# Attention's rounds and tail, the first expert slots in a new order, and 16-bit routing tables built from pairs

## The chip, the cores and the metric

The kernel runs on one core of a Trainium2 chip. The metric is the device time of one execution in microseconds (us); three runs of the kernel before gave 990.22, 992.68 and 995.25, median 992.68. In the profile PE is TensorE (PEld its weight loads), DVE is VectorE, ACT is ScalarE, POOL is GpSimd, and SP is SyncE, which issues most of the loads.

## What is computed

Three layers follow each other. Attention over 4 batches, 8 heads of 64 and 768 positions: each chunk of 32 queries sees 16 keys to its left, itself, 8 to its right, and 8 memory keys. Its output, 3072 tokens of 512, goes to a mixture of experts with one expert per token, and that to a dense layer.

```python
scores = scale * q_c @ concat([mem_k, k_ctx]).T        # per chunk of 32 queries
a = exp(scores - scores.max(-1)); a = a / (a.sum(-1) + 1e-9)
out[chunk] = a @ concat([mem_v, v_ctx])
x = out.reshape(3072, 512)
logits = (x / (|x| + 1e-6)) @ (emb / (|emb| + 1e-6)).T / tau     # 8 experts
e = logits.argmax(1); g = softmax(logits)[e]
y = g * (relu(x @ w1[e]) @ w2[e])                      # w1 512x1024, w2 1024x512
r = relu(y @ w_in); out = (r * r) @ w_out              # w_in 512x2048
```

## The kernel before

The order of every engine's instructions is written by hand: the code emits them in the order in which each engine takes them, and each engine works through its own queue in that order. DMAs are issued by SP, POOL and ACT as instructions of their queues.

Attention runs in 32 rounds (4 batches, 4 pairs of heads, 2 halves), as a pipeline over the stages in `order`. In round i come stage_b(i), the scores in `sp` (two banks in turn); max_b, sub_b and exp_b(i); stage_c(i-1), which transposes the probabilities in `ps_t` and copies them to `pt`; stage_d(i-2), times v, in the one bank `ps_o`; inv_d and scale_d(i-2), which empty it into `xa`; stage_t(i-3), which stores a half batch to x_d at its last pair of heads, and transposes `xa`; stage_m(i-4), the logits `lp`; and stage_u(i-5), which at the last pair transposes the logits (`dp`, in `ps_t`) into `dots`. `windows` lays out keys on POOL two rounds ahead. v, k and q are loaded on SP three, five and four pairs ahead. Five more rounds without new scores end the attention.

`early` is a generator whose steps run behind the stages: after each of batches 0 to 2 it chooses an expert per token (choose, five DVE ops), then picks the fullest expert, finds its first 256 tokens by one-hot tables (`ohs`, `rid`, product `ip`) and gathers them as slots 0 and 1. `begin` loads that expert's first weights as soon as it is known. `routing` (steps "N") counts all tokens and builds the rest: positions, one-hot tables osl, rid, ohl, the ids of the other slots by the product `idp` (31 slots of 128 tokens), experts and reloads, gates ("M", "rgm", product `gp`) and scatter indices.

Products in the slots split each operand into a high part (ACT copy) and a low part (DVE subtraction), and use three matmuls. Letters in the strings given to `run` name steps: W splits a weight block, x transposes and splits tokens, a and b are the two halves of the first product (12 matmuls each, with ReLU on ACT), c and d transpose their results, e and f are the halves of the second product, G gathers, V renews a weight block if the expert changes, F scales and scatters a slot, q takes squares of x for the norm, p is a quarter of an opened a.

```python
x0 x1 q | A0 p q W1 q | p q p q | N q q q p          # rounds 33 to 36; W0 in 32
N2 p9 N3 a1 c0 b0 N4 W2 d0 b1 N5 G2 G3 W3 N6 e0 c1 N6 f0 M4 d1 x2 N6 R V0 V1 G4 e1 M99 N7 f1 a2 x3 b2 N8 c2 F0 F1 V2 N9 V3 N10
```

After these a loop takes slots 2 to 27, two stages apart, with the dense layer's weights converted in between (its first steps: a3, d2, e2, c3, x4, b3, f2). The dense layer follows from about 480 us on.

Of the kernel before, what the change touches and what calls it, by code (L numbers as in the profile page):

```python
# [21 lines left out]
def kernel(  # L22
# [196 lines left out]
    def attention(actx, hooks, space, drain):  # L219
        x_p = actx.enter_context(tc.tile_pool(name="x", bufs=4))  # L220
# [100 lines left out]
        def stage_d(i):  # L321
            b, hp, half = ks[i]
            pt = st.pop(i)
            vt, c0 = vb[i // 2 % NV], i % 2 * NC
            op = ps_o.tile([P, HT, 2, D + 1], F32, name="op", tag="o")
            for c in range(NC):
                j = c % 4
                nc.tensor.matmul(
                    out=op[32 * j:32 * j + 32, c // 4],
                    lhsT=pt[:, c // 4, 32 * j:32 * j + 32],  # L330
                    rhs=vt[:, :, c0 + c, :],
                    start=True, stop=True,
                    tile_position=(0, 32 * j),
                )
            st[i] = op
# [18 lines left out]

        def stage_t(i):
            b, hp, half = ks[i]
            xa = x_t[b, half]
            if hp == HP - 1:
                T0 = (2 * b + half) * HT
                nc.gpsimd.dma_start(out=x_d[T0 * P:(T0 + HT) * P, :].rearrange("(t p) d -> p t d", p=P), in_=xa)  # L360
# [7 lines left out]
        def stage_m(i):  # L368
# [9 lines left out]
            if hp == HP - 1:  # L378
                lt = wk.tile([32 * HT, P], F32, name="lt", tag="lt", bufs=2)
                copy("a", lt, lp[half])  # L380
                st[i] = lt

        def stage_u(i):
            b, hp, half = ks[i]
            if hp == HP - 1:
                lt = st.pop(i)
                dp = ps_t.tile([P, HT, P], F32, name="dp", tag="t")[:, 0, :32 * HT].rearrange("p (t e) -> p t e", e=32)
# [39 lines left out]
        clear_kw(0, nc.vector)  # L427
        clear_kw(1, nc.scalar)
# [25 lines left out]
        cst = {"scratch": scratch}  # L454
        chores = {
            0: [
                start_en, lambda: windows(1), lambda: clear_kw(2, nc.scalar),
                lambda: [f(j) for f, j in ((load_q, 1), (load_k, 2), (load_q, 2), (load_k, 3), (load_q, 3), (load_k, 4))],
            ],
            4: [finish_en],  # L460
            8: [lambda: cst.update(routing_consts(route, per))],
        }
        later = {
            0: [lambda: clear_v(1, 0, nc.scalar), lambda: load_v(1)],
            1: [lambda: clear_v(2, 0, nc.scalar)],
            2: [lambda: clear_v(2, 1, nc.scalar), lambda: load_v(2)],
            3: [lambda: clear_v(3, 0, nc.scalar)],
            4: [lambda: clear_v(3, 1, nc.scalar), lambda: load_v(3)],
            5: [lambda: clear_v(4, 0, nc.scalar)],
            6: [lambda: clear_v(4, 1, nc.scalar), lambda: load_v(4), lambda: load_v(5)],  # L470
# [19 lines left out]
        for i in range(NK + LAG + 3):  # L490
            if i == NK:
                qk_ctx.close()
                space()
            for f in chores.get(i, []):
                f()
            for f, lag in order:
                if lag <= i < NK + lag:
                    f(i - lag)
                if stage_of(i):
                    wait[0] = next(early, None) == 1  # L500
                drain((i - NK, order.index((f, lag))))
# [12 lines left out]
            drain((i - NK, -1))  # L514
            for _ in range(min(len(squares), 1 if i < NK else 0)):
# [4 lines left out]
        while vec:  # L520
            vec.pop(0)()
        for f in squares:
            square(*f)
        for _ in early:
            pass
        return cst


    def routing_consts(pool, tmp):
        c = {}  # L530
# [3 lines left out]
        nc.vector.tensor_copy(out=c["iota"], in_=it[:, 0:NS])  # L534
        itp = tmp.tile([P, 1], I32, name="itp")
        nc.gpsimd.iota(itp, pattern=[[0, 1]], base=0, channel_multiplier=1)
        c["p"] = pool.tile([P, 1], F32, name="p_f")
        nc.vector.tensor_copy(out=c["p"], in_=itp)
        c["p1"] = pool.tile([P, 1], F32, name="p1_f")
        nc.vector.tensor_scalar(out=c["p1"], in0=c["p"], scalar1=1.0, scalar2=None, op0=ALU.add)  # L540
        c["rev"] = pool.tile([P, E], F32, name="rev")
        nc.vector.tensor_scalar(
            out=c["rev"], in0=c["iota"][:, 0:E], scalar1=-1.0, scalar2=float(E), op0=ALU.mult, op1=ALU.add
        )
        c["iota_b"] = pool.tile([P, P], BF16, name="iota_b")
        nc.vector.tensor_copy(out=c["iota_b"], in_=it)
        c["ones"] = pool.tile([P, P], BF16, name="ones_b")
        nc.vector.memset(c["ones"], 1.0)
        c["first"] = pool.tile([P, E], F32, name="first")
        nc.vector.tensor_copy(out=c["first"], in_=c["rev"])  # L550
        nc.vector.memset(c["first"][:, 0:1], float(E * 2 * NT))
        c["upper"] = pool.tile([P, P], BF16, name="upper_b")
# [3 lines left out]
        return c  # L556
# [36 lines left out]
    def early(c, per, ps, begin, gather):  # L593
# [47 lines left out]
        for T in range(TE - 1):  # L641
# [17 lines left out]
        lf = t([P, TE], BF16, "lf")  # L659
        nc.vector.scalar_tensor_tensor(  # L660
            out=lf, in0=osl[:, :, 1], scalar=-float(P), in1=pe, op0=ALU.mult, op1=ALU.add
# [19 lines left out]
        yield from gap((6, 1, 6, 1, 8, 6)[4])  # L681
# [17 lines left out]

    def routing(rp, c):  # L700
        def t(shape, dt=F32, name=None, tag=None):
            return rp.tile(shape, dt, name=name, tag=tag or name)

        def gates(g, gb):
# [20 lines left out]
            for j in range(3):  # L725
                nc.vector.tensor_copy(out=gb[j], in_=g)
                yield
                if j < 2:
                    nc.vector.tensor_tensor(out=g, in0=g, in1=gb[j], op=ALU.subtract)
# [21 lines left out]
        for _ in choose(c, rp, TE, NT):  # L751
            pass
        turn(c, rp, km[:, TE:NT].rearrange("p t o -> p (t o)"), "1")
        for _ in tally(c, rp, 1):
            pass
        g = t([P, NT, 1], name="g")
        gb = [t([P, NT, 1], BF16, name=f"gb{j}") for j in range(3)]
# [7 lines left out]
        yield  # L765
        for part in range(2):
# [49 lines left out]
        lo = t([P, NT, 1], BF16, name="lo")  # L816
        nc.vector.tensor_copy(out=lo, in_=posi)
        slot = t([P, NT, 1], name="slot")
        nc.vector.tensor_copy(out=slot, in_=sli)
        osl = t([P, NT, NS], BF16, name="osl")  # L820
        nc.vector.tensor_tensor(
            out=osl, in0=c["iota"][:, 0:NS].unsqueeze(1).to_broadcast([P, NT, NS]),
            in1=slot.to_broadcast([P, NT, NS]), op=ALU.is_equal,
        )
        rid = t([P, NT, 2, NS], BF16, name="rid", tag="rid")
        nc.vector.tensor_tensor(
            out=rid[:, :, 0, :], in0=osl,
            in1=c["iota"][:, 0:NT].unsqueeze(2).to_broadcast([P, NT, NS]), op=ALU.mult,
# [3 lines left out]
        idp = ps_r[2].tile([P, 2, NS], F32, name="idp", tag="o")  # L832
        yield
        nc.vector.tensor_tensor(
            out=ohl, in0=c["iota_b"].unsqueeze(1).to_broadcast([P, NT, P]), in1=lo.to_broadcast([P, NT, P]),
            op=ALU.is_equal,
        )
# [5 lines left out]
        nc.scalar.activation(out=idt, in_=idp[:, 0, :], func=ACTF.Copy, scale=float(P))  # L843
        nc.vector.tensor_tensor(out=ida, in0=idt, in1=idp[:, 1, :], op=ALU.add)
        nc.vector.tensor_scalar(out=gid[:, KE:NS], in0=ida[:, KE:NS], scalar1=-1.0, scalar2=0.0, op0=ALU.add, op1=ALU.max)
        rg = t([P, NT, 3, NS], BF16, name="rg")

        def rgm(j):
            nc.vector.tensor_tensor(out=rg[:, :, j, :], in0=osl, in1=gb[j].to_broadcast([P, NT, NS]), op=ALU.mult)
# [66 lines left out]
        gp = ps_r[1].tile([P, 3, NS], F32, name="gp", tag="t")  # L916
# [806 lines left out]
```

## Time and profile before

| | us |
|---|---|
| median of three runs | 992.68 |
| the profiled execution | 992.88 |
| its span, first to last instruction | 991.2 |
| PE busy | 952.7 (96%) |
| DVE busy | 622.8 (63%) |
| ACT busy | 396.8 (40%) |
| POOL busy | 161.4 (16%) |

The mean granted clock of TensorE is 0.991 of its full speed. "Busy" is the time in which an engine works at all; the time between the span and the execution's own time, 1.7 us, is start and end. The stretches in which the change lies are the first sixth of the span: the rounds up to the start of round 29 (91.49), the end of attention up to the first expert product (113.64), and the first slots up to slot 2's second product (160.58).

### The profile page before, as it was taken

Reading aid. Unit: us, or ns where it says so; the run is one execution under the profiler, and the core shown is the slowest. Engines: PE = TensorE matmul, PEld = TensorE weight load, DVE = VectorE, ACT = ScalarE, POOL = GpSimd, SP = SyncE. Lnnn points to the kernel's source line nnn. Section 1 sums busy time; section 2 is a strip of 40 time slices with the busy share of each in tenths; the row PEclk is TensorE's granted clock in tenths of the full one; section 3 lists DMA queues with packets and bytes.
Section 4 is the critical chain, followed back from the end, with each engine's and each line's share of the span. In section 5 each row is a group of like instructions: output and inputs, shape, how many; then the busy total and the mean of one; then the engine's idle time right before and its main releaser. Section 6 shows DMA issues by size and latency. Waiting matters only on the chain.

```text
span 991.2 us, 17171 instructions
## 1 busy us (share of the span) xinstructions
PE 952.7 (96%) x5982; PEld 775.9 (78%) x5982; DVE 622.8 (63%) x1259; ACT 396.8 (40%) x731; POOL 161.4 (16%) x197
## 2 busy tenths in 40 slices
PE   6889799999999999999899999999999999999997
PEld 5767577888887887878688888878888888888886
DVE  7778795647757677877798645555454555444522
ACT  7656533635546465666432213421111341111221
POOL 8765212121211111110000001010000101000011
PEclk9999899999999999999999999999999999999999
DMA  8994716554857676896565434032454204224011
GB/s 322 350 411 146 254 42 229 193 166 130 309 183 280 210 276 239 317 342 233 184 203 192 161 123 143 1 110 85 145 191 146 88 1 151 91 100 148 1 43 43
DMA packets 62496, 172.94 MB, mean 174 GB/s; under 512 B 7092, under 2 KB 7220, under 8 KB 62400
## 3 DMA queue, kind: packets, MB, share of 16 engines
q1 hardware_dynamic: 43392, 122.45, 35.5%
q0 software_dynamic: 8640, 28.32, 8.0%
q10 hardware_dynamic: 10368, 20.98, 6.2%
q8 instruction: 49, 0.80, 0.3%
q14 instruction: 47, 0.39, 0.1%
HBM read 213.66 MB, written 38.80 MB: 255 GB/s over the span
## 4 chain that ended last, share of the span: by engine, by line
issue 66%; DMA 15%; POOL 2%; POOLq 0%
DMA y_d<-ysb,sidx 15%; POOL out_dram L1382 2%; POOLq L1719 0%; POOLq L1031 0%; POOLq L1382 0%; POOLq L1157 0%; POOLq L1656 0%; POOLq L1665 0%
## 5 line engine op out<-in xcount | busy, mean ns | idle before, releaser
L1357 PE MATMUL acc<-wo,g 128*128 128x512 f32 x384 | 151.2, 394 | 0.2
L1359 PE MATMUL acc<-wo,g 128*128 128x512 f32 x384 | 151.0, 393 | 0.0
L1358 PE MATMUL acc<-wo,g 128*128 128x512 f32 x384 | 149.5, 389 | 0.0
L1382 POOL DMA_INDIRECT out_dram<-osb,oid x24 | 23.6, 983 | 483.9 <-ACT osb L1378 355.9
L1359 PEld LDWEIGHTS acc<-wo,g 128*128 128x128 f32 x384 | 72.1, 188 | 17.3 <-DVE g L108 1.3
L1357 PEld LDWEIGHTS acc<-wo,g 128*128 128x128 f32 x384 | 72.1, 188 | 16.5 <-ACT g L105 1.5
L1358 PEld LDWEIGHTS acc<-wo,g 128*128 128x128 f32 x384 | 72.2, 188 | 16.0
L1402 DVE SCALAR_TENSOR_TENSOR cf<-cf 128x512 f32<-128x512 f32 x54 | 37.1, 692 | 75.7 <-ACT cf L1425 74.9
L1157 POOL DMA_INDIRECT y_d<-ysb,sidx x28 | 32.2, 1150 | 273.4 <-ACT ysb L1156 214.7
L105 ACT CAST g<-cf 128x512 fp32r<-128x512 f32 x54 | 33.6, 622 | 106.9 <-PE acc L1359 71.0
L1425 ACT COPY cf<-zX 128x512 f32<-128x512 f32 x24 | 14.1, 586 | 155.2 <-PE zX L1336 155.2
L1336 PE MATMUL zX<-yc,ww 128*128 128x512 f32 x192 | 68.8, 399 | 2.3 <-DVE tu L1291 2.3
L108 DVE TENSOR_TENSOR g<-gk,g 128x512 fp32r<-128x512 f32 x42 | 29.1, 692 | 66.3 <-ACT g L105 66.3
L1336 PE MATMUL zW<-yc,ww 128*128 128x512 f32 x192 | 68.2, 396 | 0.4 <-PEq L1665 0.4
L1336 PE MATMUL zY<-yc,ww 128*128 128x512 f32 x192 | 67.7, 393 | 0.0
L105 ACT CAST g<-gk 128x512 fp32r<-128x512 f32 x42 | 26.2, 623 | 79.8 <-PE acc L1359 79.8
L108 DVE TENSOR_TENSOR g<-cf,g 128x512 fp32r<-128x512 f32 x54 | 37.4, 692 | 29.8 <-ACT g L105 28.9
L135 POOL COPY kw<-kt 64x672 f32<-64x672 f32 x62 | 51.3, 828 | 10.2 <-PE sp L277 7.8
L108 DVE TENSOR_TENSOR hTlb<-tr,hThb 128x512 fp32r<-128x512 f32 x28 | 19.3, 690 | 44.0 <-ACT hThb L105 43.6
L1108 PE MATMUL yps<-wh2a,hTha 128*128 128x512 f32 x112 | 46.2, 413 | 0.0
L1336 PEld LDWEIGHTS zX<-yc,ww 128*128 128x128 f32 x192 | 36.6, 190 | 10.9 <-ACT ysb L1156 2.7
L1108 PE MATMUL hps<-wh1b,xT 128*128 128x512 f32 x104 | 43.2, 415 | 1.8 <-ACT ha L1125 1.8
(328 smaller groups left out, 2281.2 us busy)
## 6 DMA issues: line engine op xcount, KB each, us to landing
ww<-wi_d SPq DMA_DIRECT2D x77, 512.0 KB
r1a<-in_moe_w_dram SPq DMA_DIRECT2D x54, 512.0 KB
r1b<-in_moe_w_dram SPq DMA_DIRECT2D x54, 512.0 KB
r2a<-in_moe_w_dram SPq DMA_DIRECT2D x52, 512.0 KB
r2b<-in_moe_w_dram SPq DMA_DIRECT2D x52, 512.0 KB
wi_d<-ww SPq DMA_DIRECT2D x28, 512.0 KB
vb<-in_v_dram SPq DMA_DIRECT2D x32, 390.0 KB
rw<-in_moe_w_in_dram ACTq DMA_DIRECT2D x32, 256.0 KB
```

Source lines behind the costliest of these rows:

```text
L105: nc.scalar.copy(out=hi, in_=src)
L108: eng.tensor_tensor(out=lo, in0=src, in1=hi.bitcast(F32), op=ALU.subtract)
L135: (nc.vector if eng == "v" else nc.gpsimd).tensor_copy(out=out, in_=in_)
L1108: nc.tensor.matmul(out=out_ps, lhsT=ah, rhs=wh, start=first, stop=False)
L1157: nc.gpsimd.indirect_dma_start(out=y_d[:, :], out_offset=bass.IndirectOffsetOnAxis(ap=sidx[:, s:s + 1], axis=0), in_=y, in_offset=None, bo ...
L1336: nc.tensor.matmul(out=z, lhsT=w[:, d % 2, wx, kt], rhs=y[yx][:, kt, :], start=start and (kt, x) == (0, 0), stop=(kt, x) == (1, 2), skip_g ...
L1357: nc.tensor.matmul(out=self.acc[j], lhsT=g[:, 0, c], rhs=wt[:, 0], start=first, stop=False)
L1358: nc.tensor.matmul(out=self.acc[j], lhsT=g[:, 0, c], rhs=wt[:, 1], start=False, stop=False)
L1359: nc.tensor.matmul(out=self.acc[j], lhsT=g[:, 1, c], rhs=wt[:, 0], start=False, stop=last)
L1382: ins = nc.gpsimd.indirect_dma_start(out=out[:, :], out_offset=bass.IndirectOffsetOnAxis(ap=oid[:, jj:jj + 1], axis=0), in_=o, in_offset=N ...
L1402: nc.vector.scalar_tensor_tensor(out=o, in0=x, scalar=0.0, in1=x, op0=ALU.max, op1=mul)
L1425: nc.scalar.copy(out=c1[:, 0], in_=z)
```

## The change

In the rounds, the choices for batches 0 and 1 run one step per round instead of one per stage; the constants of the routing become a generator, two steps a round; `dp` goes to the pool of `lp`; v of pair 1 is loaded ahead of four other loads and v of pairs 2 to 5 one round earlier; six x tiles instead of four, and batch 1 is stored after rounds 27 and 28. Stage_d of round 30 uses `sp`'s first bank. Attention's last rounds are written out, with the weights' high (h, j, H) and low parts (l, k, L) as steps of their own, and transposes (X, C, D) apart from their splits (Y and y, g, i). One-hot tables read index and position as pairs of 16-bit words, and their inner width grows from 31 to 32. The first slots come in a new order: b0 and b2 have PSUM banks of their own, `gp` comes behind d2, and y2 has its bank held ahead. Slot 3's a and slot 2's d move out of the loop into the string.

```diff
-            sp = (ps_s, ps_s2)[i % 2].tile([P, HT, 64, 2], F32, name="sp", tag="s")
+            sp = (ps_s, ps_s2)[i % 2].tile([P, HT, D + 1, 2], F32, name="sp", tag="s")[:, :, 0:64]
-            op = ps_o.tile([P, HT, 2, D + 1], F32, name="op", tag="o")
+            pool, tag = (ps_s, "s") if i == NK - 2 else (ps_o, "o")
+            op = pool.tile([P, HT, 2, D + 1], F32, name="op", tag=tag)
-                dp = ps_t.tile([P, HT, P], F32, name="dp", tag="t")[:, 0, :32 * HT].rearrange(...)
+                dp = ps_l.tile([P, HT, 32], F32, name="dp", tag="l")
+        clear_v(1, 0, nc.scalar)
-                lambda: [f(j) for f, j in ((load_q, 1), (load_k, 2), (load_q, 2), (load_k, 3), (load_q, 3), (load_k, 4))],
+                lambda: [f(j) for f, j in ((load_q, 1), (load_k, 2), (load_v, 1), (load_q, 2), (load_k, 3), (load_q, 3), (load_k, 4))],
+            27: [lambda: store(1, 0)],
+            28: [lambda: store(1, 1)],
-            return not wait[0]
+            return not wait[0] and (i >= starts[-1] or f is stage_u)
+                if i > 4 and f is stage_u:
+                    for _ in range(2):
+                        next(consts, None)
+                if (i, f) == (NK - 1, stage_c):
+                    drain("h0")
...
+        L = NK - 1
+        drain("h1")
+        stage_d(L - 1)
+        for _ in range(3):
+            next(early)
+        stage_m(L - 3); stage_c(L); stage_t(L - 2); inv_d(L - 1); scale_d(L - 1)
+        drain("l0 q q")
+        stage_d(L); stage_m(L - 2); stage_t(L - 1); inv_d(L); scale_d(L)
+        drain("l1 j0")
+        stage_m(L - 1, False); stage_t(L)
+        drain("X0")
+        for _ in early: pass
+        finish_m(L - 1); stage_m(L); stage_u(L - 1)
+        drain("Y0")
+        stage_u(L)
+        drain("y0")
+        # choose, turn and tally of the last batch
+        drain("N q q j1 A0 p2 X1 k0 Y1 y1 k1 q p9 q")
...
-                out=all_ohs[:, T:T + G], in0=c["iota_b"].unsqueeze(1).to_broadcast([P, G, P]),
-                in1=lf[:, T:T + G].unsqueeze(2).to_broadcast([P, G, P]), op=ALU.is_equal,
+                out=paired(all_ohs[:, T:T + G]), in0=along(c["iota_b"], G), in1=across(lf[:, T:T + G], P),
+    def paired(t):
+        return t.rearrange("p t (a b) -> p t a b", b=2)
+    def along(row, n):
+        m = row.shape[1]
+        return row.rearrange("p (a b) -> p a b", b=2).unsqueeze(1).to_broadcast([P, n, m // 2, 2])
+    def across(col, m):
+        return col.unsqueeze(2).to_broadcast([P, col.shape[1], m // 2, 2])
-        yield from gap((6, 1, 6, 1, 8, 6)[4])
+        yield from gap(12)
...
+            pool, tag = {(0, "b"): (self.ps_y, "y"), (2, "b"): (ps_r[0], "s")}.get((s, ab), (self.ps_h, self.tags[0]))
-        run("N2 p9 N3 a1 c0 b0 N4 W2 d0 b1 N5 G2 G3 W3 N6 e0 c1 N6 f0 M4 d1 x2 N6 R V0 V1 G4 e1 M99 N7 f1 a2 x3 b2 N8 c2 F0 F1 V2 N9 V3 N10")
+        run("N a1 c0 H20 H21 b0 N L20 L21 N b1 d0 e0 C1 H30 H31 L30 N G2 G3 L31 g1 f0 D1 N i1 e1 N x2 N R f1")
+        run("V0 V1 G4 a2 M12 x3 M99 b2 N c2 N V2 a3 d2 N O2 F0 F1 V3 N N")
```

The tables osl, rid, ohl and rg use `paired`, `along` and `across` in the same way.

## Rows read from the trace of the kernel before

**Rows 1.** Busy us and count of each engine by stretch, PEclk, DMA share, GB/s.
```profile
0.00:91.49 91.49, 76.75 (x1666) 60.84 (x1666) 69.57 (x230) 62.29 (x134) 68.59 (x109) 1.00 0.88 333
91.49:113.64 22.15, 15.65 (x306) 12.31 (x305) 18.45 (x61) 11.43 (x27) 5.26 (x8) 0.92 0.46 156
113.64:160.58 46.94, 42.02 (x248) 32.40 (x248) 38.92 (x113) 18.83 (x37) 6.06 (x8) 0.93 0.49 168
160.58:480.00 319.42, 312.92 (x1544) 259.17 (x1543) 225.64 (x409) 181.93 (x316) 57.43 (x51) 1.00 0.69 239
480.00:991.20 511.20, 505.38 (x2224) 411.19 (x2223) 270.20 (x449) 122.28 (x221) 24.05 (x25) 0.99 0.32 107
```
**Rows 2.** PE's waits from 0 to 91.49: total us, times, longest.
```profile
PE op L328 <- issue: 2.4, 3, 1.2
PE op L328 <- ACT xt L133: 1.3, 1, 1.3
PE dp L388 <- ACT pt L133: 1.2, 5, 0.2
PE op L328 <- DVE mx L293: 1.1, 1, 1.1
PE op L328 <- DVE sp L288: 0.7, 1, 0.7
```
**Rows 3.** Timeline of weight loads near 19.7: start, us, operation, idle before and releaser.
```profile
19.71 0.63 PEld L328 LDWEIGHTS op<-vb,pt 128*32 128x32 f32 x24 [1.31 <-ACT xt L133]
```
**Rows 4.** Stretches of 5 us in the rounds, columns of rows 1.
```profile
60.00:65.00 5.00, 3.85 (x69) 2.71 (x66) 3.48 (x10) 2.94 (x10) 4.70 (x8) 1.00 1.02 412
...
80.00:85.00 5.00, 5.00 (x121) 4.11 (x120) 3.88 (x12) 3.35 (x9) 3.78 (x6) 1.00 0.52 193
```
**Rows 5.** Timeline of DVE: first and last operation of the first choice.
```profile
44.17 0.20 DVE L563 TENSOR_REDUCE mxl<-dots 128x6 f32<-128x48 f32 x1
...
45.95 0.47 DVE L611 TENSOR_TENSOR e_o<-rev,km 128x48 bf16<-128x48 f32 x1
```
**Rows 6.** DVE groups from 91.49 to 160.58: busy us, mean ns, idle before.
```profile
L834 DVE TENSOR_TENSOR ohl<-iota_b,lo 128x3072 bf16<-128x3072 bf16 x1 | 3.3, 3348 | 0.0
...
L669 DVE TENSOR_TENSOR scratch<-iota_b,e_lf 128x768 bf16<-128x768 bf16 x3 | 2.8, 950 | 0.1
L849 DVE TENSOR_TENSOR rg<-osl,gb 128x744 bf16<-128x744 bf16 x3 | 2.6, 927 | 0.0
L108 DVE TENSOR_TENSOR wl1a<-r1a,wh1a 128x1024 fp32r<-128x1024 f32 x2 | 2.4, 1224 | 1.9 <-ACT wh1a L105 1.9
L108 DVE TENSOR_TENSOR wl1b<-r1b,wh1b 128x1024 fp32r<-128x1024 f32 x2 | 2.4, 1223 | 2.2 <-ACT wh1b L105 2.2
...
L826 DVE TENSOR_TENSOR rid<-osl,iota_f 128x744 bf16<-128x744 bf16 x1 | 0.9, 939 | 0.0
...
L830 DVE TENSOR_SCALAR rid<-osl,p_f 128x744 bf16<-128x744 bf16 x1 | 0.4, 406 | 0.0
```
**Rows 7.** Timeline of PE in attention's end and the first slots.
```profile
104.35 1.52 PE L328 MATMUL op<-vb,pt 128*32 128x130 f32 x24 [1.08 <-ACT xt L133]
...
151.50 0.69 PE L1108 MATMUL hps<-wh1b,xT 128*128 128x512 f32 x1 [1.82 <-ACT ha L1125]
...
155.96 1.23 PE L918 MATMUL gp<-rg,ohl 128*128 128x93 bf16 x24
...
160.58 0.48 PE L1108 MATMUL yps<-wh2a,hTha 128*128 128x512 f32 x1
```
**Rows 8.** DVE's busy us from the end of round 31 to the gate tables.
```profile
104.25:155.49 51.24, 42.38 (x120) 0.90 0.47 157
```
**Rows 9.** PE's waits from 91.49 to 160.58, as in rows 2.
```profile
PE hps L1108 <- ACT ha L1125: 2.6, 2, 1.8
...
PE xp L363 <- DVE spare L108: 1.7, 1, 1.7
PE ip L684 <- DVE e_rid L680: 1.3, 1, 1.3
```

More of the change, by code (lines that the diff above doesn't have):

```diff
@@ L353, in square, with store @@
             nc.scalar.activation(out=sq, in_=x_t[b, half][:, t, :], func=ACTF.Square, accum_out=ssq[:, T:T + 1])
+        def store(b, half):
+            T0 = (2 * b + half) * HT
+            nc.gpsimd.dma_start(out=x_d[T0 * P:(T0 + HT) * P, :].rearrange("(t p) d -> p t d", p=P), in_=x_t[b, half])
         def stage_t(i):
@@ L357, in stage_t @@
             xa = x_t[b, half]
-            if hp == HP - 1:
-                T0 = (2 * b + half) * HT
-                nc.gpsimd.dma_start(out=x_d[T0 * P:(T0 + HT) * P, :].rearrange("(t p) d -> p t d", p=P), in_=xa)
+            if hp == HP - 1 and b != 1:
+                store(b, half)
             tp = ps_a.tile([P, HT, P], F32, name="xp", tag="a")
@@ L366, in stage_t, with finish_m, stage_m @@
             st[i] = xt
-        def stage_m(i):
+        def finish_m(i):
+            lt = wk.tile([32 * HT, P], F32, name="lt", tag="lt", bufs=2)
+            copy("a", lt, lp[ks[i][2]])
+            st[i] = lt
+        def stage_m(i, finish=True):
             b, hp, half = ks[i]
@@ L377, in stage_m @@
                 )
[L378 to L381, printed above, removed]
+            if hp == HP - 1 and finish:
+                finish_m(i)
         def stage_u(i):
@@ L489, in attention @@
         cst["square"] = lambda: square(*squares.pop(0)) if squares else None
[L490 to L493, printed above, removed]
+        for i in range(NK):
             for f in chores.get(i, []):
@@ L750, in routing @@
         stp = ps_r[1].tile([P, E], F32, name="stp", tag="t")
[L751 to L755, printed above, removed]
         g = t([P, NT, 1], name="g")
-        gb = [t([P, NT, 1], BF16, name=f"gb{j}") for j in range(3)]
+        gb = [t([P, NT, 2], BF16, name=f"gb{j}") for j in range(3)]
         gate_ops = gates(g, gb)
@@ L831, in routing @@
         ohl = t([P, NT, P], BF16, name="ohl")
-        idp = ps_r[2].tile([P, 2, NS], F32, name="idp", tag="o")
+        idp = ps_r[2].tile([P, 2, NP], F32, name="idp", tag="o")
         yield
[L834 to L837, printed above, removed]
+        nc.vector.tensor_tensor(out=paired(ohl), in0=along(c["iota_b"], NT), in1=across(lo, P), op=ALU.is_equal)
         yield
@@ L915, in routing @@
         yield
-        gp = ps_r[1].tile([P, 3, NS], F32, name="gp", tag="t")
-        for T in range(NT):
-            nc.tensor.matmul(out=gp, lhsT=ohl[:, T, :], rhs=rg[:, T], start=(T == 0), stop=(T == NT - 1))
-        nc.vector.tensor_reduce(
-            out=gate.unsqueeze(2), in_=gp.rearrange("p j s -> p s j"), op=ALU.add, axis=AX.X
-        )
         nc.vector.tensor_tensor(
@@ L946, in routing @@
         yield
-        eq = t([P, NT, NS], name="eq", tag="rid")
+        gp = ps_r[1].tile([P, 3, NP], F32, name="gp", tag="t")
+        for T in range(NT):
+            nc.tensor.matmul(out=gp, lhsT=ohl[:, T, :], rhs=rg[:, T], start=(T == 0), stop=(T == NT - 1))
+        nc.vector.tensor_reduce(
+            out=gate.unsqueeze(2), in_=gp[:, :, 0:NS].rearrange("p j s -> p s j"), op=ALU.add, axis=AX.X
+        )
+        yield
+        eq = t([P, NT, NP], name="eq", tag="rid")[:, :, 0:NS]
         nc.vector.tensor_tensor(
@@ L989, in first, with first_high, first_low @@
             self.after(kind, 0)
+        def first_high(self, i, kind="1a"):
+            nc.scalar.copy(out=self.res[kind][i][0], in_=self.raw[kind, i])
+        def first_low(self, i, kind="1a"):
+            hi, lo = self.res[kind][i]
+            nc.vector.tensor_tensor(out=lo, in0=self.raw[kind, i], in1=hi.bitcast(F32), op=ALU.subtract)
+            if i:
+                self.after(kind, 0)
         def renew(self, kind, s, eng="v"):
@@ L1103, in xtr @@
                 lo = self.sp.tile([P, KD, P], F32R, name="xTl", tag="xTl")
-            split(hi, lo, tp)
+            parts = [
+                lambda: nc.scalar.copy(out=hi, in_=tp),
+                lambda: nc.vector.tensor_tensor(out=lo, in0=tp, in1=hi.bitcast(F32), op=ALU.subtract),
+            ]
+            if apart:
+                self.parts[s] = parts
+            else:
+                for f in parts:
+                    f()
             self.xT[s] = (hi, lo)
@@ L1140, in mm2 @@
             hh, hl = self.hT.pop((s, ab))
-            if ab == "a":
+            if ab == "a" and s not in self.y:
                 pool, tag = (ffn.ps, "zW") if s % 2 and KE < s < NA - 3 else (self.ps_y if s else self.ps_y0, "y")
```

142 lines of the change are left out of this document (93 added, 49 removed).

## The prediction, made before the result was known

> **What bounds the kernel now.** I read the windows first [rows 1]. From 160.58 us on TensorE is busy all but 6.5 us of 319, at full clock, and the same holds near enough to the end: there only fewer matmuls would help, and the change takes none away. What can be gained lies ahead of 160.58, the start of slot 2's second product, a point that both orders reach with the same PE work done. PE idles 14.7 us of the 91.49 of the rounds, 6.5 of the 22.15 of attention's end and 4.9 of the 46.94 of the first slots; in the last two the mean clock is 0.92 and 0.93, so about 3.5 and 6.6 us ran at the lower of the two levels (1.2 instead of 2.4 GHz). VectorE (DVE) is the next engine there: 38.92 of 46.94 us busy.
>
> The waits of PE in the rounds [rows 2] name what holds them: the single PSUM bank of stage_d's output, which scale_d has to empty first, so that DVE's lateness shows as PE's wait (1.3 and 0.7 us); the logit transpose `dp`, which shares its bank with the probability transposes (1.2 in five places); 1.1 us under DVE `mx`, at 19.75, where the weight load ahead of it shows ACT's `xt`, long done by then [rows 3], so that I read it as the v tile still in flight; and 2.4 us of "issue" in the middle of groups of stage_d, where nothing in the profile is waited for, while the DMA engines were full [rows 4]. The 1.3 us wait comes right behind the choice: its operations begin at 44.17, the last at 45.95 [rows 5], in front of the round's max.
>
> **Part by part: the rounds.** For batches 0 and 1 the choice becomes one DVE operation at the end of each round from 12 on (the last, from round 28, stays dense), and the constants two a round. That takes 1.3 and 0.7 off [rows 2]; I count 1.8. A new op costs about 0.2 there; DVE idles 21.9 of 91.49 us [rows 1], 0.65 a round, so it hides; without that cover, ten choice steps and eleven constants would cost some 4 us. `dp` in lp's bank no longer waits for the copy of `pt`: 1.2. The v load for pair 1 goes ahead of four q and k loads on SP's in-order queue, and its zeros ahead of the first windows on ACT: 1.1, of which I count 0.9, since scale_d is next late; four q and k tiles land two transfers' time later, and bounds are a gain of 1.1 and, if one of them is then late, a loss of as much. The store of batch 1 moves on POOL's queue past some thirty window copies to rounds 27 and 28; ahead of it POOL no longer waits for scale_d, and 1.6 MB leave the stretch with a DMA share of 1.02 for one with 0.52 [rows 4]. If the "issue" gaps are late instruction loads they shrink; bounds are 0 and 2.4, and I take the middle, 1.2, because one gap coincides with a choice and one does not. Sum of the rounds: 1.8 + 1.2 + 0.9 + 1.2 = 5.1 us; bounds -1.1 and 6.6.
>
> **The tables from pairs.** Before, every table row is built at the one-element rate: 3348 ns for 3072 elements, 927 to 950 for 744 or 768 [rows 6]. No two-source operation at another rate is in this trace, so the ends are no gain and the rate of the nearest all-16-bit row, `rid` by a scalar: 744 elements in 406 ns, 44% of the two-source row. I take a half, near that row, since both read pairs of 16-bit words side by side: ohl 1.6, osl and rid 0.4 each, rg 1.2 saved of the slots, 3.6 together, and 1.2 of the three early tables.
> The Trainium skill (VectorE: DVE Perf Modes, section on the perf-mode tier table) gives two-tensor operations on 16-bit SBUF data twice the base rate and no more; by it these four groups would save the 4.8 us that I take, by the other reading nothing; no row here shows it.
>
> **Attention's end and the first slots.** The three early tables stand in front of max and sub of round 31, and the ids of the first gathers follow: 1.2 us earlier. Stage_d of round 30 gets a bank of its own and no longer waits 1.08 [rows 7]. That brings the first expert product forward by 2.3.
> From 104.25 to 155.49 DVE is one long queue, 42.38 busy of 51.24 [rows 8]. Its two largest gaps, 1.9 and 2.2, are waits for the high halves that ACT was just then making [rows 6]; now h, j and H stand far ahead of l, k and L, with other DVE work between. Off go 4.1 of gaps and 3.6 of tables. Added is the low half of x3, which moves ahead of the gates: 0.6, half of a 1024-wide row [rows 6]. DVE side: 7.1 shorter, 1.2 earlier, 8.3 in all.
> On PE the gate product `gp` waits for DVE's last tables. It stood before c2, a3 and d2, some 3.5 us of work (gp 155.96 + 1.23 to 160.58 [rows 7]); now these run while DVE finishes. DVE and order together: 11.8.
> The PE bound is lower. In 113.64 to 160.58 PE is busy 42.02; with the 6.6 us at the lower level run at full clock that is 38.7, so 8.2 can go there, and with the 2.3 ahead of it 10.5. The waits that would go are named [rows 9]: 2.6 for ReLU results in the one bank of the first products (b0 and b2 now have banks of their own), one of them the 1.82 before 151.50 [rows 7]; 1.7 for x's halves, 1.3 for `ip`. I count 9.5, a microsecond below the bound, for small waits that come back.
> What is moved in and could wait: h0 stands in front of the last exp on ACT and needs the first weights, loaded in round 30; the gathers stand ahead of the stores of batch 3 and of the 2a and 2b loads on POOL, and these come earlier with it; L20 and L21 stand in front of the one-hot table on DVE and put off the ids of gathers 2 and 3 by 2.4 (two rows of 1.22), covered by f0 and e1, which now run before x2; if that cover is short, up to 2.4 are lost. The copies of y0 and y1 come later, which only their banks feel: y2 gets one of its own.
>
> **Sum.** 5.1 + 9.5 = 14.6. The profiled execution took 992.9 (span 991.2), next to the median of 992.7: 992.9 - 14.6 = 978.3, forecast 978 us. Its own bounds: all waits of the rounds and the full PE bound give 6.6 + 10.5, 976; PE's busy time holds ends that are modelled, so I allow 4 more below.
>
> **Rivals.**
> Tables at the old rate: 4.8 comes back on DVE, 11.8 becomes 7.0, less the microsecond 6.0: 992.9 - 11.1 = 982. For it: the second source still steps by zero over the middle axis. 0.10.
> The clock falls anyway. Before 104.35 PE did a few small groups with gaps of 1.3 [rows 9] and 1.1, and the 24 small matmuls there took 1.52; at 151.50, after 1.82 idle behind a full run, a matmul took 0.69 against 0.48 at 160.58 [rows 7]. The new end of attention still goes from engine to engine, with transposes between. If the slow share stays, 3.3 of the PE bound is not recovered, and the end of attention is longer by about one: 982. The Trainium skill (TensorE: Matmul & The Clock Gate, part 4 on transposes) says that transposes do not count as busy for the clock as matmuls do; by that rule attention's end, with its many transposes, would be at the lower level; the rounds, with the same mix, show 1.00 [rows 1], which speaks against it. 0.14.
> DMA holds the rounds. With a share of 1.02 [rows 4] faster rounds may only wait for q, k and v; the rounds give 1: 982. Against: the loads run three to five pairs ahead, and the waits of the rounds show one late tile [rows 2]. 0.10.
> Two of these together: 986 to 990, mostly no change. 0.09.
> Slower: DVE becomes what the first slots wait for, and PE's gaps, each as long as the 1.82 before 151.50, recur in every block, so that the clock stays at the lower level through them. Eleven blocks of 12 matmuls by 0.21 each (0.69 - 0.48 [rows 7]) are 28 us. It decides from 70 of the 132 matmuls on, where the 14.6 are used up; at 90% of them 978 + 25 = 1003. Against it: DVE's queue is shorter than before by 7, and PE has four blocks of products between the waits. 0.07.
>
> **How the numbers follow.** The forecast has 0.50. Within 0.5% (988 to 998) is about what a measurement of this kernel can tell from no change. Faster: forecast, old table rate, clock, DMA, 0.84; the same 0.09; slower 0.07. The range 972 to 987 holds the forecast's bounds and the three single rivals and leaves out the slower one, most of the double ones and a little below.
>
> **What would show it.** Right: ohl near 1.7 us; `dp` and stage_d without waits in rounds 12 to 24; first hps near 111 on a clock of 5 us earlier, so 106 in the span; no gap of DVE over a microsecond until rg but the branch at V0; gp right behind d2; slot 2's second product starting near 146 instead of 160.58. Wrong: a wait of PE over 1.5 us behind DVE low halves after b0, granted clock 0.50 after the first hps, stage_b waiting for q or windows, or a stretch after 160.58 that is longer than before, which the sum takes as unchanged.

## The result, and the profile after

The changed kernel takes 978.24 us (median of 4, 975.62 to 983.58) against 993.81 (990.22 to 995.25): a ratio of 0.9846, 95% interval 0.9817 to 0.9875. The forecast was 978. The total came out as forecast, several of the steps under it did not. The windows of the changed kernel, cut at the same events as [rows 1] (columns as there):

```profile
0.00:87.46 87.46, 75.32 (x1666) 60.17 (x1666) 67.90 (x230) 61.71 (x133) 66.52 (x106) 1.00 0.91 339
87.46:107.26 19.80, 15.80 (x330) 11.89 (x329) 17.84 (x63) 14.06 (x33) 10.17 (x14) 1.00 0.63 219
107.26:149.67 42.41, 39.18 (x231) 31.18 (x227) 35.91 (x112) 16.41 (x32) 3.76 (x4) 0.96 0.54 185
149.67:480.00 330.33, 324.99 (x1600) 268.80 (x1597) 234.84 (x427) 185.81 (x322) 57.18 (x51) 1.00 0.67 233
480.00:976.80 496.80, 491.35 (x2171) 400.35 (x2169) 260.95 (x432) 118.65 (x213) 23.62 (x24) 1.00 0.32 109
```

Round 29's `sp` starts 4.03 us earlier (forecast 5.1), the first expert product 6.38 (107.26; forecast 106), slot 2's second product 10.91 (149.67 for 160.58; forecast 146). From there to the end of the span it is 827.1 us instead of 830.6, where the sum had no change. So 3.7 us were missing at slot 2's second product, 1.1 of them already at round 29 and 2.6 behind it (6.9 gained there, forecast 9.5), and 3.5 came back after that product.

PE's waits in the rounds, beside [rows 2] (total us, times, longest):

```profile
PE tp L316 <- ACT e L305: 1.7, 1, 1.7
PE op L329 <- ACT sq L354: 1.4, 1, 1.4
PE op L329 <- issue: 1.2, 1, 1.2
PE sp L277 <- issue: 0.9, 1, 0.9
PE op L329 <- DVE sp L288: 0.4, 2, 0.2
```

The waits of `dp` and most of those behind DVE are gone; three stalls of about a microsecond are left (under ACT `sq` and twice under "issue"; the last section says where they stand), and the wait for the first exponential (1.1 in the kernel before) is 0.6 longer, because ACT now clears 1560 words for the second v tile ahead of the first keys. The tables on DVE, beside [rows 6]:

```profile
L891 DVE TENSOR_TENSOR ohl<-iota_b,lo 128x3072 bf16<-128x3072 bf16 x1 | 1.8, 1751 | 0.0
L721 DVE TENSOR_TENSOR scratch<-iota_b,e_lf 128x768 bf16<-128x768 bf16 x3 | 1.6, 550 | 0.1
L903 DVE TENSOR_TENSOR rg<-osl,gb 128x768 bf16<-128x768 bf16 x3 | 1.5, 556 | 0.5 <-DVEq L1066 0.5
```

They run at a little over half of the old time. And PE in the first slots, from c2's transposes to slot 2's second product (start, us, operation, idle before and its releaser), where [rows 7] has 151.50 to 160.58:

```profile
140.69 0.60 PE L1211 MATMUL tr<-ident,ha 128*128 128x128 f32 x4
141.89 0.50 PE L1186 MATMUL hps<-wh1a,xT 128*128 128x512 f32 x1 [0.60 <-ACTq L1066]
143.97 0.50 PE L1187 MATMUL hps<-wl1a,xT 128*128 128x512 f32 x1 [1.58 <-DVEq L1066]
...
145.34 0.63 PE L1186 MATMUL hps<-wh1a,xT 128*128 128x512 f32 x1
...
148.67 1.18 PE L999 MATMUL gp<-rg,ohl 128*128 128x96 bf16 x24
149.67 0.47 PE L1186 MATMUL yps<-wh2a,hTha 128*128 128x512 f32 x1
```

Here is what the forecast left out. The product a3, the first of slot 3, was moved ahead of `gp`; its weights are renewed under a condition (`If`, L1066), which ACT and DVE evaluate in their queues at the place where `use` of the next product, b2, issues it. That place is behind the gate's operations (M99). PE waits 0.60 for ACT to reach it and 1.58 for DVE, though nothing is renewed (no split of the 1a weights runs on either engine there); then a matmul takes 0.63 instead of 0.39 until `gp`.

### The profile page after: what moved, and what is told of

It is laid out like the page before. It is cut to its first block, busy times and chain, and to the rows that moved or that the text cites. A ratio compares the mean times of both kernels' runs of the same rounds, so it can differ in the third digit from the quotient of the medians.

```text
span 976.8 us, 17175 instructions
## 1 busy us (share of the span) xinstructions
PE 946.6 (97%) x5982; PEld 772.4 (79%) x5982; DVE 617.4 (63%) x1260; ACT 396.6 (41%) x731; POOL 161.2 (17%) x197
## 4 chain that ended last, share of the span: by engine, by line
issue 37%; PE 12%; POOL 2%; POOLq 0%; DVE 0%; ACT 0%; ACTq 0%
PE zW L1422 2%; PE zX L1422 2%; POOL out_dram L1468 2%; PE zY L1422 2%; PE acc L1445 1%; PE acc L1443 1%; PE acc L1444 1%; PE zZ L1422 1%; POOLq L1813 0%; POOLq L1468 0%; DVE g L108 0%; ACT g L105 0%; ACTq L105 0%
## 5 line engine op out<-in xcount | busy, mean ns | idle before, releaser
L1188 PE MATMUL yps<-wh2a,hTla 128*128 128x512 f32 x112 | 44.2, 395 | 0.0
```

The lines of the kernel that those rows point to most:

```text
L1188: nc.tensor.matmul(out=out_ps, lhsT=al, rhs=wh, start=False, stop=last)
```

## Experiments

Beside each group of experiments the kernel before ran on the same chip (medians 993.55 to 994.80), and the ratios are to those runs. The points in the span, in us (e2 is the start of slot 2's second product; n is the number of timed executions):

| kernel | sp of round 29 | first hps | e2 | sp 29 to e2 | e2 to end | time | n |
|---|---|---|---|---|---|---|---|
| before | 91.49 | 113.64 | 160.58 | 69.09 | 830.6 | 993.81 | 4 |
| after | 87.46 | 107.26 | 149.67 | 62.21 | 827.1 | 978.24 | 4 |
| after_again | 86.82 | 107.27 | 147.88 | 61.06 | 827.6 | 979.75 | 4 |
| if_first | 87.22 | 107.70 | 146.57 | 59.35 | 829.4 | 978.64 | 4 |
| if_v2 | 85.78 | 106.73 | 145.91 | 60.13 | 828.8 | 976.22 | 4 |
| one_elem | 87.70 | 109.30 | 153.81 | 66.11 | 831.5 | 983.48 | 4 |
| pairs_only | 92.40 | 113.93 | 158.33 | 65.93 | 830.2 | 989.38 | 10 |
| a3_loop | 87.23 | 107.74 | 151.60 | 64.37 | 829.2 | 982.75 | 4 |
| dense | 88.96 | 109.95 | 150.65 | 61.69 | 827.0 | 979.25 | 1 |
| dp_old | 89.34 | 110.50 | 152.84 | 63.50 | 827.6 | 982.11 | 1 |
| v_late | 88.61 | 109.54 | 150.37 | 61.76 | 830.3 | 982.31 | 1 |
| op30_old | 85.93 | 107.97 | 149.94 | 64.01 | 829.6 | 981.20 | 1 |
| if_v2_vlate | 87.71 | 108.60 | 147.93 | 60.22 | 828.3 | 977.98 | 4 |
| if_v2_zeros | 86.05 | 106.50 | 145.53 | 59.48 | 828.1 | 975.83 | 4 |

Seven of these have the changed kernel's rounds unaltered (after, after_again, if_first, if_v2, one_elem, a3_loop, op30_old): their round 29 starts at 85.78 to 87.70, mean 86.88. That width is the error bar of a single profile there. Behind round 29 two profiles of the changed kernel differ by 1.15 (62.21 and 61.06).

**if_first: the branch ahead of the gate.**

```
-V0 V1 G4 a2 M12 x3 M99 b2 N c2 N V2 a3 d2 N
+V0 V1 G4 a2 M12 x3 b2 M99 N c2 N V2 a3 d2 N
```

> The changed kernel with slot 2's second half of the first layer (b2) issued ahead of the rest of the gate's operations instead of behind them, so that the conditional renewal of slot 3's 1a weights, which b2's use emits on ACT and DVE, is decided before them. Theory: of the 3.7 us by which slot 2's second product starts later than forecast (149.67 for 146), 2.2 are the two waits of slot 3's first half (0.60 on ACT's branch, 1.58 on DVE's) and 1.5 the lower clock behind them. Expected: neither wait over 0.3, granted clock 1.00 from 140 to 150, the second product at 146.0 to 147.3 (gp may now wait up to 1.4 for rg, since the gate's exponential comes behind hb on ACT), the time 975 to 976. Rival: the wait is on what the branch decides (a weight load or its flag) and not on its place in the queue; then the product stays at 149 or later and the time at 978.

Its timeline of PE, columns as above:

```profile
141.27 0.48 PE L1186 MATMUL hps<-wh1a,xT 128*128 128x512 f32 x1
141.59 0.39 PE L1187 MATMUL hps<-wl1a,xT 128*128 128x512 f32 x1
...
145.57 1.18 PE L999 MATMUL gp<-rg,ohl 128*128 128x96 bf16 x24 [0.85 <-DVE rg L903]
146.57 0.47 PE L1186 MATMUL yps<-wh2a,hTha 128*128 128x512 f32 x1
148.46 0.50 PE L1187 MATMUL yps<-wl2a,hTha 128*128 128x512 f32 x1 [1.42 <-DVEq L1066]
```

a3 loses both waits, the granted clock is 1.00 from 140 to 150, `gp` waits 0.85 for rg, and e2 is at 146.57, all as expected: the wait was the branch's place in the queue. But the time is 978.64 (ratio 0.9848, 0.9805 to 0.9890), where 975 to 976 was expected. The next branch, V2 for slot 2's 2a weights, stood behind cmpt to sidx on DVE and now holds e2's second matmul 1.42.

**if_v2: the second branch, too.**

```
-V0 V1 G4 a2 M12 x3 M99 b2 N c2 N V2 a3 d2 N
+V0 V1 G4 a2 M12 x3 b2 M99 N V2 c2 N a3 d2 N
```

> As if_first (slot 2's b2 issued ahead of the rest of the gate's operations), and the renewal of slot 2's 2a weights (V2) moved from behind the output indices (cmpt to sidx on DVE) to right behind rg. In if_first a3 lost its waits and slot 2's second product began at 146.57, but its second matmul then waited 1.42 us on DVE's branch of V2 (148.46). Theory: that branch, too, is late only by its place; expected: second matmul by 147.2 with no wait over 0.3, 1.3 us less than if_first in the second matmul's start, the clock 1.00 to 150, the time 976 to 977, or 1.3 below if_first beside it. Rival: V2's branch waits for a weight load or for its flag, and the wait stays at 148 wherever it is put (rg's reader gp then comes later, too): no gain, time as if_first or longer.

```profile
144.91 1.18 PE L999 MATMUL gp<-rg,ohl 128*128 128x96 bf16 x24 [0.86 <-DVEq L1066]
145.91 0.48 PE L1186 MATMUL yps<-wh2a,hTha 128*128 128x512 f32 x1
146.22 0.40 PE L1187 MATMUL yps<-wl2a,hTha 128*128 128x512 f32 x1
```

There is no wait behind e2, the second matmul starts at 146.22, and the time is 976.22 (0.9820, 0.9799 to 0.9841). e2 is 14.67 earlier than in the kernel before, as forecast (14.6), but 5.7 of that are a round 29 that is the earliest of the seven, 1.1 ahead of their mean. What the branches decide is the part behind round 29: the forecast gave 9.5 there, the changed kernel gains 6.9 and 8.0 (after_again), and the four kernels with the first or both branches moved gain 8.9 to 9.7.

**one_elem: tables read one element at a time, in the new order.**

```
-        return t.rearrange("p t (a b) -> p t a b", b=2)
+        return t
-        return row.rearrange("p (a b) -> p a b", b=2).unsqueeze(1).to_broadcast([P, n, m // 2, 2])
+        return row.unsqueeze(1).to_broadcast([P, n, m])
-        return col.unsqueeze(2).to_broadcast([P, col.shape[1], m // 2, 2])
+        return col[:, :, 0:1].to_broadcast([P, col.shape[1], m])
```

> The changed kernel with the tables' operands read as in the kernel before: one element held with step 0 along the inner axis instead of two (paired, along and across give plain views; types and sizes stay). Theory of the forecast: the tables go back to their full time (ohl 3.3 us, early tables 0.93 each, rg 0.9 each, rid 0.9) and DVE bounds the end of attention and the first slots, so first hps is about 1 us later and slot 2's second product 3.5 to 4.8 later (153.2 to 154.5); time 982. Rival: in the new order TensorE's own work and the branch bound that stretch, and the tables cost less than 2 us of the second product's start; time 979 to 980.

Its table of DVE groups and PE's first group behind the biggest table:

```profile
L891 DVE TENSOR_TENSOR ohl<-iota_b,lo 128x3072 bf16<-128x3072 bf16 x1 | 3.4, 3351 | 0.0
L721 DVE TENSOR_TENSOR scratch<-iota_b,e_lf 128x768 bf16<-128x768 bf16 x3 | 2.8, 947 | 0.1
```

```profile
127.73 0.87 PE L894 MATMUL idp<-rid,ohl 128*128 128x64 bf16 x24 [1.18 <-DVE ohl L891]
```

Types and sizes are those of the changed kernel, so the step-0 element alone costs the factor of two. Counted from round 29, e2 is 3.9 later than in the changed kernel (66.11 - 62.21), 5.1 later than in after_again; the time is 983.48 (0.9880, 0.9836 to 0.9923). The forecast's 4.8, of which it counted a microsecond less on the path, fits both. One profile can't say more: it is of the slowest of the four executions (986.99), with a granted clock of 0.92 from round 29 to the first hps, where the changed kernel has 1.00.

**pairs_only: the pairs alone, in the kernel before** (the helpers above, pieces, flags and tile numbers in pairs; nothing else).

> The kernel before with the pairs alone (tables' operands, gate pieces and flags in pairs; order, banks, choices and consts as before). Theory of the forecast: DVE bounds from the early tables to rg, so the 4.8 us that the tables save are all on the path: first hps 1.2 earlier (112.4), slot 2's second product 4.0 to 4.8 earlier (155.8 to 156.6), time 989. Rival: without the new order other waits (gathers, xp behind squares, ha) take the room: the product less than 2.5 us earlier, time 991 or more.

The biggest table, ohl, takes 1748 ns here, too, and e2 is 3.16 earlier from round 29 (69.09 - 65.93), 2.25 in the span. The time is 989.38 (0.9950, 0.9927 to 0.9974). The time is the first theory's, the point lies between the two. The point is mixed with the clock, too: from the first hps to e2 it is 2.5 shorter, but there the granted clock is 1.00 instead of 0.93, and PE is busy 38.42 instead of 42.02. In the old order a part of what DVE saved met another wait, stage_d's last op for `pt` (0.16 in the kernel before, at 107.75):

```profile
108.12 1.40 PE L328 MATMUL op<-vb,pt 128*32 128x130 f32 x24 [2.14 <-ACT pt L133]
```

**a3_loop: a3 and d2 behind gp again** (out of the string, and the two `if s > KE` of the loop removed).

> The changed kernel with slot 3's first half (a3) and the second transposes of slot 2 (d2) back behind gp, as in the kernel before. The forecast gave 3.5 us to this order, as work that fills gp's wait for rg. Theory: most of that was eaten by the branch: gp now waits 3 to 4 us for rg (ready near 145.5), a3 and d2 follow without a wait of their own, and slot 2's second product starts at 150 to 151 against 149.67; time 979. If the forecast's 3.5 was right the product starts at 153 or later and the time is 981.5. Rival: the branch cost more than the order gave; the product starts before 149.3 and the time is below 978.

```profile
145.82 1.89 PE L999 MATMUL gp<-rg,ohl 128*128 128x96 bf16 x24 [4.27 <-DVE rg L903]
```

`gp` waits 4.27, longer than either theory had, and its 24 matmuls take 1.89 instead of 1.18, at a granted clock of 0.66 from 145 to 150. e2 is at 151.60, between the 150 to 151 of mine and the 153 of the forecast's step; time 982.75 (0.9881, 0.9841 to 0.9922), nearer to that step's 981.5. From round 29 the order is worth 2.2 to 3.3 us with its branch wait (64.37 less 62.21 and 61.06) and 4.2 without it (less 60.13). But a part of a3_loop's own delay is the clock: from `gp` to e2 it takes 5.78, where the kernel before takes 4.25 for the same work (160.58 - 155.96, less 0.37 for c2). With these 1.5 off, an estimate, the order is worth 1.8 with its branch wait (beside after_again) and 2.7 to 3.5 without it (beside if_v2 and if_first). My theory that the branch had eaten most of it is not borne out: it took a third to a half.

**dense: choices in a row and constants at once** (`return not wait[0]`; all constants in round 8).

> The changed kernel with the choices of the first three batches in a row again and the routing constants at once in round 8, as in the kernel before. Theory of the forecast: 1.2 to 1.8 us come back as waits of op and dp behind DVE in rounds 8 to 20, round 29's sp at 88.7 to 89.3 against 87.2 to 87.5 in the three runs of the changed rounds. Rival: the other edits left DVE with room, or the waits were put down to DVE but had another cause; then less than 0.4.

```profile
47.59 0.87 PE L329 MATMUL op<-vb,pt 128*32 128x130 f32 x24 [1.53 <-ACT xt L133]
...
71.70 0.87 PE L329 MATMUL op<-vb,pt 128*32 128x130 f32 x24 [1.85 <-ACT xt L133]
```

Round 29 starts at 88.96, 1.3 to 3.2 behind the seven, 2.1 behind their mean: as forecast (1.2 to 1.8), within what one profile tells. The first stall stands at the same product as the 1.35 of the kernel before (48.54), behind the choice of batch 0. The second stands behind the choice of batch 1, one round later than a stall of 1.25 under "issue" in the kernel before (71.09). The row names ACT's xt, but DVE's division xa, which empties op's one bank and comes behind the choice in DVE's queue, ends at 71.60 (71.04 and 0.56), and op starts at 71.70.

**dp_old: dp in tp's bank again** (`ps_t`, tag "t").

> The changed kernel with dp back in the bank of tp. Theory of the forecast: tp of the next round waits for DVE's copy of dots, and dp for ACT's pt: 1.2 us by round 29's sp (88.4 to 88.8 against 87.2 to 87.5), with dp's idle time near 0.2 each in its eight rounds. Rival: the time only moves between waits of one round; round 29's sp less than 0.4 later.

```profile
39.60 0.30 PE L395 MATMUL dp<-ident,lt 96*128 96x96 f32 x1 [0.24 <-ACT pt L133]
```

There are six such rows up to 89.11, 1.4 together, and round 29 starts at 89.34, 2.5 behind the mean (1.6 to 3.6). The rounds with a dp are 0.25 to 0.46 longer from sp to sp than in if_first (3.02 for 2.56 in four of the six), 2.5 together: twice the forecast's term.

**v_late: v's second load behind q and k, its zeros behind the first round, the loads of pairs 2 to 5 a round later.**

> The changed kernel with v's second load behind q and k again and its zeros after the first round, as in the kernel before. Theory: the early zeros on ACT hold the first exponential 0.6 (10.46 for 9.85) and the late load holds op 1.1 (near 20); so the first exponential at 9.85, the wait at 20 again 1.0 to 1.3, and round 29's sp 0.4 to 0.5 later than in the other runs (87.6 to 88.0). Rival of the forecast: the early zeros cost nothing and the load is worth 0.9 or more: 88.1 or later. Second rival: the wait at 20 is no wait for v and stays out: 86.7 to 86.9.

The first exponential, and the op that waited 1.07 in the kernel before:

```profile
9.85 0.52 ACT L305 ACTIVATE e<-e 128x384 f32<-128x384 f32 x1 [1.15 <-DVE e L301]
```

```profile
18.57 0.87 PE L329 MATMUL op<-vb,pt 128*32 128x130 f32 x24 [0.33 <-DVE enT L459]
...
38.63 0.51 PE L277 MATMUL sp<-kw,q 128*32 128x128 f32 x9 [2.07 <-issue]
```

The zeros' cost on ACT is confirmed (9.85 for 10.46), and the wait at 19.75 does not come back, though the load is issued where it was: the prediction had taken that wait for v's load without proof. Round 29 is late all the same (88.61), from a stall of 2.07 at 38.63 inside a group of sp, with the clock at 0.50 for two microseconds behind it.

**if_v2_vlate and if_v2_zeros: the start, on top of if_v2** (the first with v_late's edit; the second with `clear_v(1, 0, nc.vector)` behind `windows(0)`).

> if_v2 with v's second load and its zeros where the kernel before has them (as v_late). In v_late the first exponential came at its old time and the wait of op near 20 stayed out, but a stall of 2.07 at 38.6, with the clock at 0.59 behind it, took more than that back. Theory: that stall is chance, as the stalls inside groups of op differ by run; round 29's sp then 0.5 to 1.2 earlier than the 87.1 that the five runs with the new rounds have as their mean (85.9 to 86.6), time 975.3 to 976.0. Rival: v's loads, all one round later, cause the stall near 38; round 29's sp at 88.3 or later, time 978 or more.

> if_v2 with the early zeros of v's second buffer on DVE, behind its copies of mkT, instead of on ACT ahead of the keys' copies; the early load of v stays. Theory: the first exponential was 0.6 late because ACT had 1.49 more ahead of it; it comes at 9.85 to 10.0, and round 29's sp is 0.4 to 0.7 earlier than the mean of 87.1 (stalls inside op's groups aside); time 975.5 to 976.0. Rival: DVE's 1.36 push the first row maximum instead, exponential at 10.4 or later and no gain; time as if_v2.

With v late there is no stall at 38, so the rival falls; but the first exponential comes at 10.60, because the expert table landed 1.2 later than in the kernel before (ACT's square of it at 6.87 for 5.70), and round 29 at 87.71 shows no gain. Time 977.98 (0.9842, 0.9824 to 0.9860). With the zeros on DVE the exponential comes at 11.02: that rival was right, and round 29 at 86.05 is inside the seven. Time 975.83 (0.9821, 0.9802 to 0.9840), the same as if_v2. What the early load of v is worth stays open.

**op30_old: round 30's op in the shared bank.**

> The changed kernel with round 30's op back in the one bank that the other op have. Theory of the forecast: it waits for DVE's division of the op before it, 1.08 in the kernel before; from round 31's sp to the first hps it takes 13.6 to 14.8 where the runs with the new order take 12.6 to 13.75. Rival: the new order has other work there, and less than 0.3 comes back; then no later than 13.75, and the step that the forecast named was already hidden.

```profile
98.42 0.87 PE L329 MATMUL op<-vb,pt 128*32 128x130 f32 x24 [1.86 <-ACT e L305]
```

It waits 1.86, where the changed kernel shows 0.24 (98.32). From round 31's sp to the first hps it is 14.80 us, against 13.2 in after_again, if_first and if_v2_zeros (12.6 in the changed kernel's first profile): 1.6, the step named, larger than its 1.08. A part can be the clock, 0.50 from 100 to 102 behind that wait.

**after_again: the changed kernel once more.**

> The changed kernel itself once more, beside if_v2's variants on the same chip. What repeats is an effect, what does not is chance. Expected to repeat: slot 3's waits on the branch (0.6 on ACT, 1.6 on DVE) with the lower clock behind them, slot 2's second product 62.2 to 62.9 after round 29's sp, ohl at 1.75. Expected not to repeat: the place and length of the stalls inside the groups of op (round 29's sp anywhere in 86 to 88.5), and the 827.1 from the second product to the end, which lay between 827 and 831.5 in ten profiles of either order; time 977 to 979.

The branch waits repeat to 0.01 (0.60 and 1.57), ohl and the rest, too. The lower clock behind them does not: e2 comes 61.06 after round 29's sp, not 62.2 to 62.9, and from the second matmul of a3 to e2 it is 4.10 us instead of 5.70 (143.97 to 149.67):

```profile
143.78 0.50 PE L1187 MATMUL hps<-wl1a,xT 128*128 128x512 f32 x1 [1.57 <-DVEq L1066]
...
147.88 0.48 PE L1186 MATMUL yps<-wh2a,hTha 128*128 128x512 f32 x1
```

So the 3.7 us that I had put down to the branch were three things: 1.1 were missing at round 29 already, 1.6 were the clock of that execution, and the branch's own part is smaller than its two waits of 2.2. From the first hps to e2 after_again takes 40.61 and the four kernels with the branch moved 38.87 to 39.33: 1.3 to 1.7, since `gp` then waits 0.85 to 1.04 for rg or for the moved branch. (The three add up to a little over 3.7, because without the branch this stretch gains 7.6 to 8.1, more than the 7.2 that the forecast had for it.) The time is 979.75 (0.9861, 0.9842 to 0.9880). On the same chip if_v2_zeros is 0.4% faster, with intervals that do not meet, and if_v2_vlate 0.2%, with intervals that overlap: **with both branches moved the kernel is 0.2 to 0.4% faster than the changed one**. if_v2 itself ran on another chip; its ratio there is that of if_v2_zeros (0.9820 and 0.9821), so no gain of the zeros is seen, and if_v2 is the version to keep.

## Why the prediction was right, and where not

- **The rounds, 5.1.** They gave 4.0 in the changed kernel, 4.6 in the mean of the seven. Choice and constants gave 2.1 (1.8 named) and dp 2.5 (1.2), less 0.6 for the zeros on ACT, which the prediction listed and priced at nothing. The 0.9 for v's load is not shown; the later store of batch 1 and the two x tiles more were not run by themselves. The 1.2 for "issue" failed: stalls of 1.6 to 3.4 us in all stay in the seven, and their places have nothing to do with the choice (see the last section). The bounds of the rounds add up to 6.5 at the top, not 6.6.
- **Tables, 4.8 on DVE.** They were right in size and rate. On the path they are worth 3.9 to 5.1 in the new order (one_elem) and 3.2 in the old (pairs_only), each with a part of the clock in it. That the order helps the tables, by taking away the waits that would take their place, is not shown by so small a difference. The rule cited from the Trainium skill (VectorE: DVE Perf Modes, perf-mode tier table) agrees: 3348 to 1751 ns for two 16-bit sources. What it needs here is that both words of a pair are read side by side; a step-0 element keeps the old rate (3351) at the same types, as ohl did in the kernel before, where both its sources were 16-bit already [rows 6].
- **DVE's gaps, 4.1, and round 30's bank, 1.08.** The gaps are gone from the trace, though no run puts the weights' old order back; the bank's 1.08 is 1.6 in op30_old. Until rg DVE has no gap over a microsecond but the 1.14 at V0 and V1's branch, as the prediction said.
- **The step that failed: "now these run while DVE finishes".** Of c2, a3 and d2, a3 could not, because its weights hang on a branch that DVE only reaches behind the work that a3 was to cover. The prediction counted the instructions that moved, and not the renewal that the next `use` issues with them. It cost 2.2 of waits, 1.3 to 1.7 of them on the path to e2, and in three of the six profiles with these waits and the tables from pairs another 1.3 to 1.6 by the clock (from a3's second matmul to e2 5.44 to 5.70 in after, dp_old and op30_old, 4.08 to 4.10 in after_again, dense and v_late). The 9.5 that the prediction counted behind round 29 come out (8.9 to 9.7) once the branch is out of the way.
- **Unchanged behind slot 2's second product.** It was 3.5 less, and that is within what single profiles differ by: the fourteen profiles give 827.0 to 831.5 for the same work, with both ends among the kernels with the new order (mean 828.9). A part is the clock: in the kernel before PE is busy 7.41 of the 10 us from 470 and the granted clock is 0.86 from 480 to 490; in the changed one it is busy 7.74 from 460 to 470 and stays at 1.00. (if_v2_zeros stays there after 7.43, so the busy time alone does not decide it.) So the total of 978 was hit with luck, by two errors of opposite sign. With the mean of all fourteen the span of after would be 978.6 and the time 980.3; after_again gives 979.75.
- **Rivals.** Old table rate: out. DMA holds the rounds: out as priced (the rounds gave 4.0, not 1; dense and dp_old show what held them), though the stalls that are left stand where the DMA engines are full. The clock: 1.00 in attention's end and 0.96 in the slots of the changed kernel, but of the twelve kernels with the new order six have 0.79 to 0.94 from 104 to 112, and four of these at 0.79 need 0.5 more from round 31's sp to the first hps (13.7 for 13.2): neither gone nor worth the 4 us of the rival. The other six have 1.00 there with the same transposes; the rule on transposes from the Trainium skill (TensorE: Matmul & The Clock Gate, part 4) would have made all twelve alike, so it does not decide here. Slower: out.

## What to carry over

When an operation is moved forward, list what its operands hang on in every queue, conditional blocks with it: a branch that does nothing still stands in line, and its place decides when the next engine may start. Move the branch ahead of the long run of work first, then what needs it; and look for the next branch at once, which takes the wait over (1.42 here, where 2.2 had gone).
Judge a step at an event in the trace that both orders reach, not at the total: 1 to 4 us here were chance of one execution, and a total that agrees can hide a miss of that size. Then look at the granted clock on the way to that event in both profiles, since a fall of it is worth as much as the step.

## What was not expected of the hardware

**Stalls inside a group.** In if_first six matmuls of op run, then PE stands for 0.89, and the other 18 follow, with nothing in between that they wait for:

```profile
54.69 0.42 PE L329 MATMUL op<-vb,pt 128*32 128x130 f32 x6
...
56.01 0.74 PE L329 MATMUL op<-vb,pt 128*32 128x130 f32 x17 [0.89 <-issue]
```

Each run with the new rounds has two to four such stalls between 38 and 69 us, where the DMA share is near 1; their count and length differ by run and make most of the 85.8 to 87.7. Their places do not differ. In the changed kernel they are

```profile
43.71 0.31 PE L277 MATMUL sp<-kw,q 128*32 128x128 f32 x3 [0.91 <-issue]
...
50.58 0.87 PE L329 MATMUL op<-vb,pt 128*32 128x130 f32 x24 [1.36 <-ACT sq L354]
...
57.33 0.74 PE L329 MATMUL op<-vb,pt 128*32 128x130 f32 x17 [1.17 <-issue]
```

and, counted in the trace, 721, 846 and 972 matmuls stand before them. In all twelve runs with the new order every wait of PE over 0.35 us from 30 to 88 us, but for three in dense, follows 595, 721, 846, 972, 1098 or 1224 matmuls (one or two more where `dp` is in its old bank): 125 or 126 apart, which is 256 instructions of PE's queue with weight loads and semaphore instructions counted. The kernel before has its "issue" waits at 973, 1099 and 1226. So these stalls belong to places in the program, also the one at 50.58 that the row puts down to ACT and the 2.07 of v_late, and only their length is left to chance. They may be the late instruction loads that the prediction named; the cause was not tried.

**The clock after a wait is not decided by the wait.** With the same waits of about 0.60 and 1.57 on the branch, the granted clock from 145 to 150 is 0.66 in after, 0.70 and 0.74 in dp_old and op30_old, and 1.00 in after_again, dense and v_late. In rounds 2 and 3 after_again shows, in windows of 2 us (columns as above),

```profile
12.00:14.00 2.00, 1.59 (x40) 0.97 (x28) 1.87 (x7) 2.00 (x4) 1.88 (x4) 0.77 1.00 407
14.00:16.00 2.00, 2.00 (x31) 1.55 (x31) 1.41 (x5) 1.56 (x4) 1.80 (x3) 0.50 1.03 413
```

a fall to the lower level, and a group of 24 matmuls of sp takes 1.51 there (14.88). The changed kernel's first profile shows 1.00 in both windows, yet the groups of rounds 2 and 3 took

```profile
11.87 1.51 PE L277 MATMUL sp<-kw,q 128*32 128x128 f32 x24
...
15.44 0.86 PE L277 MATMUL sp<-kw,q 128*32 128x128 f32 x24
```

so the first of these ran at the lower level, too. The trace's first record of the clock stands at 15.45 in this profile; before it the row shows 1.00 for want of a record, and the durations tell the level.
